# A list scheduler that knows of a port shared by VectorE and GpSimd, and one 1024-column tile of transposed exponentials in place of two of 512

## The chip, the cores and the metric

The kernel runs on one core of one Trainium2 chip. The metric is the time of one execution on the device in microseconds, as a median of runs. Engines are named as the profile names them: PE (TensorE's matmuls), PEld (its weight loads), DVE (VectorE), ACT (ScalarE), POOL (GpSimd), SP (SyncE, which here only issues DMAs).

## What is computed

```python
def _attn_ref(q, k, v, proj):            # 2 x 8 heads, 768 tokens, 64 wide
    q_bucket, k_bucket = ...             # signs of q @ proj and k @ proj, 6 bits
    mask = q_bucket[:, :, :, None] == k_bucket[:, :, None, :]
    scores = np.where(mask, scale * q @ k.T, -1e9)
    attn = np.exp(scores - scores.max(-1))
    return attn / (attn.sum(-1) + 1e-09) @ v

x = attention reshaped to 1536 x 512
x = ((x @ w1) * (x @ w2)) @ w3 @ w_out   # weights given in float64
out = sum over 4 experts of p[:, e] * (np.maximum(x @ w1[e], 0) @ w2[e])
```

The attention part is float32, and the products are made of pairs of a high part and a low part (fp32r), so that nearly every operand X is held as hi(X), a rounded copy, and lo(X) = X - hi(X).

## The kernel before, in words

The program is a list of operations, each with an engine, a duration in ns, the keys of those it depends on, and a priority. `emit_all` (the scheduler) plays this list through with a clock per engine: whichever engine is free first takes, of its operations whose inputs are there, the one with the lowest priority number, and the order that comes out is the order in which the instructions of each engine are written. On the chip each engine goes through its own list strictly in that order and waits on semaphores, so the table `RANK` (a shift of priority for each group of operations, in units of P = 5500 ns) and the durations decide who stands in front of whom.

The attention stage works on 48 **units**, one for 256 queries of one of 16 heads (three units per head). The operations of unit u are:

- `S` (PE): the scores of 128 queries against 768 keys, twice per unit, into one of two s_ps tiles.
- `mx` (DVE, L436): reads s_ps, writes e and a row minimum. `ex` (ACT, L439): exp, in place, with a row sum.
- `r1` (POOL, L452), `r2` (DVE, L454): the reciprocal of the sums. `en` (POOL L449; every fourth one on ACT, L448): scales e.
- `T` (PE, L470): 12 transposes of 128x128, in three pieces j = 0, 1, 2 of four, each into one bank of PSUM out of three (t_ps, 512 columns each).
- `hi` (ACT, L476) and `lo` (DVE, L478): read that bank and write the high and the low part of the piece into one of four et tiles. A bank is free again when `lo` of its piece is done.
- `pv` (PE): four matmuls per piece, into pv_ps. Then `po` (ACT) and `xa` (DVE for the first 27 units, POOL and a DMA afterwards) put the result into xa.

Besides that, for each head POOL prepares the hi and lo parts of q, k and v (`sc`, `h`, `l`, `vh`, `vl`: L360, L167, L170), PE and DVE make the bits for pairs of heads (`bm`, L386), and eight **conversions** run, one for each half of the four first weight tiles of the layer behind attention. `conv64` makes hi and lo parts out of float64 words: a load (`cl`), `ca` (ACT), then `c0` (L207), `c1` (L209), `c2` (L212), `c3` (L215) and `cd` (L220) on DVE, all of which read and write SBUF only, `ch` on ACT, and `cp` and `cq` on POOL (L170, L223). The priority of conversion n is C0 + n CP, so that they follow each other at equal steps. Their DVE operations carry durations of 400 and 700 ns in the scheduler where later conversions, which run with POOL idle, have 335 and 602.

From unit 38 on (`UF`) pieces rotate over two banks only, and the third (f_ps) takes the **filler**: eight chains of 12 matmuls of the next layer (`fm`), which need the converted weights, so that PE has work in the tail of attention. One of the chains uses s_ps. After attention the late stage runs from about 263 us to the end: matmul chains into u_ps and o_ps, 12 matmuls to a chain.

Of the kernel before, what the change touches and what calls it, by code (L numbers as in the profile page):

```python
# [25 lines left out]
    "C0": 16.68,  # L26
    "CP": 16.1,
    "S0": -239.52,
    "S1": 27.05,
    "T0": -88.98,  # L30
    "T1": -71.39,
    "T2": -86.81,
    "b0": -70.87,
    "b1": -163.79,
    "bits": -188.45,
    "en": -138.6,
    "ex0": 12.29,
    "ex1": -50.98,
    "fd": -30.85,
    "fx": -49.15,  # L40
    "hi0": -17.87,
    "hi1": -151.69,
    "hi2": -87.16,
    "ld": -138.95,
    "lo0": -71.6,
    "lo1": -482.92,
    "lo2": -138.58,
    "lv": -106.52,
    "mx0": -542.16,
    "mx1": -84.39,  # L50
    "p0": -19.19,
    "p1": -131.31,
    "pm": -135.95,
    "po": -194.17,
    "pr2": -131.6,
    "prep": 2.16,
    "pv": 12.21,
    "r1": -72.77,
    "r2": -255.45,
    "v": 13.17,  # L60
    "xa": -226.06,
    "xb": -108.68,
}
GROUP = {
# [10 lines left out]
def tile_lsh_attention_moe(ctx, tc, qk, v, projc, w1, w2, w3T, w_out, dp, e1, e2, out):  # L75
# [45 lines left out]
    APAD = 528  # L121
# [8 lines left out]
    NET = 4  # L130
    et_t = tiles(NET, [128, 2, 2, 256], "et", F32R)
# [16 lines left out]
    SEG = (slice(0, 512), slice(512, S))  # L148
    pv_ps = pp.tile([128, 512], F32, name="pv_ps")[:, 0:256]
    t_ps = tiles(3, [128, 512], "t_ps", p=pp)  # L150
# [3 lines left out]
    def mm(o, l, r, start, stop):  # L154
        nc.tensor.matmul(out=o, lhsT=l, rhs=r, start=start, stop=stop)  # L155
# [30 lines left out]
    def conv64(n, dst, half, src):  # L186
# [5 lines left out]
        def lo_():  # L192
# [7 lines left out]
        slow = (400, 700, 2700) if beside else (335, 602, 1460)  # L200
# [7 lines left out]
            ("DVE", slow[0], [("c0", n)], "c1",  # L208
# [5 lines left out]
            ("DVE", slow[0], [("c2", n)], "c3",  # L214
# [33 lines left out]
    def op(key, eng, dur, fn, deps, prio, group=None):  # L248
        keys[key] = len(ops)
        group = group or group_of(key)  # L250
        ops.append((eng, dur, fn, deps, prio + P * RANK.get(group, 0.0), group))

    def emit_all():
        succ = [[] for _ in ops]
        need = [0] * len(ops)
        for i, o in enumerate(ops):
            for k in set(o[3]):
                if k in keys:
                    succ[keys[k]].append(i)
                    need[i] += 1  # L260
        ready = [0.0] * len(ops)
        engines = sorted(LAT)
        free_at = {e: 0.0 for e in engines}
        wait = {e: [] for e in engines}
        avail = {e: [] for e in engines}
        for i, o in enumerate(ops):
            if not need[i]:
                heapq.heappush(wait[o[0]], (0.0, i))
        order = []
        while True:  # L270
            best = None
# [12 lines left out]
            while wait[e] and wait[e][0][0] <= t:
                i = heapq.heappop(wait[e])[1]
                heapq.heappush(avail[e], (ops[i][4], i))
            i = heapq.heappop(avail[e])[1]
            end = t + ops[i][1]
            free_at[e] = end
            order.append(i)  # L290
# [85 lines left out]
    def bits_of(ps, hs):  # L376
        for r in SEG:
            for i, hh in enumerate(hs):
                a = hh % 2
                hi, lo = hh_t[hh % HR], ll_t[hh % HR]  # L380
                mm(ps[:, r], pbh[:, a, :], hi[:, r], i == 0, False)
                mm(ps[:, r], pbl[:, a, :], hi[:, r], False, False)
                mm(ps[:, r], pbh[:, a, :], lo[:, r], False, i == len(hs) - 1)

    def is_pos(dst, ps, r, c=slice(0, S)):
        nc.vector.tensor_scalar(out=dst, in0=ps[r, c], scalar1=thr[r], scalar2=amp[r], op0=ALU.is_gt, op1=ALU.mult)  # L386

    def first_head():
# [6 lines left out]
        for i, (key, c) in enumerate(((("mq", 0), slice(0, 256)), (("sf", n), slice(256, S)))):  # L395
            op(key, "DVE", (330, 600)[i], lambda c=c: is_pos(lo[64:64 + PC, c], ps, q, c), [("mk", 0)], T + i, "b0")
# [17 lines left out]
    def unit(u):  # L414
# [6 lines left out]
        for t in range(2):  # L421
# [12 lines left out]
            op(("S", u, t), "PE", 690, score, [(k, hh) for k in ("mq", "mk", "k1", "k2", "k3", "dq")] +  # L434
               ([("sf", 0)] if 0 < u < NQ else []) + free_, Tt)
            op(("mx", u, t), "DVE", 873, lambda ps=ps, m=m, e=e: nc.vector.tensor_scalar(  # L436
                out=e, in0=ps[:, 0:S], scalar1=THR, scalar2=None, op0=ALU.min,
# [22 lines left out]
        for j in range(NJ):  # L460
            n = NJ * u + j
            ps, free_, tn = take_t(u)
            ps = ps.rearrange("p (a b) -> p a b", a=2)
            et = et_t[n % NET]

            def trans(j=j, ps=ps):
                for k in range(2):
# [7 lines left out]
            op(("T", u, j), "PE", 436, trans, en + free_, Tj)  # L475
            op(("hi", n), "ACT", 480, lambda ps=ps, et=et: nc.scalar.activation(out=et[:, 0], in_=ps, func=AF.Copy),  # L476
               [("T", u, j), ("pv", n - NET)], Tj)
            op(("lo", n), "DVE", 602, lambda ps=ps, et=et: nc.vector.tensor_tensor(  # L478
                out=et[:, 1], in0=ps, in1=f(et[:, 0]), op=ALU.subtract), [("hi", n)], Tj)
            keys[tn] = keys[("lo", n)]  # L480

        def pv(j):
            et = et_t[(NJ * u + j) % NET]
            for k in range(2):
                for p in range(2):
                    kt = 2 * j + k
                    mm(pv_ps, vv[:, kt, :], et[:, p, k, :], kt == 0 and p == 0, kt == NK - 1 and p == 1)
# [3 lines left out]
        for j in range(NJ):  # L491
            n = NJ * u + j
            op(("pv", n), "PE", 472, lambda j=j: pv(j), [("lo", n), ("vl", hh), ("xa" if u - 1 < XP else "po", u - 1), ("pv", n - 1)], Tp)
# [97 lines left out]
    def conv_tile(name, dst, fn, src, fp, after, T):  # L591
        for half in range(2):
# [3 lines left out]
            for eng, dur, deps, key, go in conv64(n, dst, half, fn(src, fp, half)):  # L596
                t = (RANK["C0"] + n * RANK["CP"]) * P if T is None else T
                hold = [("ex", CR[0] + CR[1] * n, 0)] if T is None and key == "cl" else []
                op((key, n), eng, dur, go, deps + after + hold, t - (1.5 * P if key == "cl" else 0))
# [544 lines left out]
```

## Time and profile before

| what | value |
|---|---|
| median of 3 runs | 982.67 us (982.36 to 983.55) |
| the profiled execution: its span, first to last instruction | 980.4 us |
| busy PE, DVE, ACT, POOL | 966.2, 718.6, 455.8, 200.4 us |
| mean granted TensorE clock | 1.000 |
| last `pv` ends, first chain into u_ps starts | 254.8 us, 263.3 us |

The span leaves out what lies before the first and after the last instruction of the program; the profiled execution has no other time of its own, and its span stands 2.3 us under the median of the runs. PE is busy nearly all the time by its row, but a matmul's end is modelled and matmuls overlap, so a busy PE may still be waiting a little; how much has to be counted from the spacing of its instructions.

### The profile page before, as it was taken

The numbers are of one execution on the slowest core, as the hardware profiler recorded it, in microseconds if no ns is written. First come the engines' busy times: TensorE is split into PE (matmuls) and PEld (weight loads), VectorE is DVE, ScalarE is ACT, GpSimd is POOL, SyncE is SP. The second block draws the span as 40 slices with busy tenths as digits, with TensorE's granted clock in tenths as the row PEclk, the third lists the DMA queues.
The fourth block names the chain that finished last, engine by engine and source line by source line (L and its number), as shares of the span: only waits on it lengthen the run. The fifth ranks groups of instructions, "written<-read, shape, count | busy, mean of one in ns | idle before, by whom it ended". The sixth has DMA issues, their size and how long they took to land.

```text
span 980.4 us, 14358 instructions
## 1 busy us (share of the span) xinstructions
PE 966.2 (99%) x5227; PEld 833.1 (85%) x5227; DVE 718.6 (73%) x1401; ACT 455.8 (46%) x864; POOL 200.4 (20%) x244
## 2 busy tenths in 40 slices
PE   8999999999999999999999999999999999999998
PEld 7999989888888888888888888888888888888886
DVE  7999999998599974964798745777457674476543
ACT  6999999987443422444543223322232322323121
POOL 6978878886100000000000000000000000000000
PEclk9999999999999999999999999999999999999999
DMA  6645444330133331330021102001021000200011
GB/s 171 184 124 137 114 105 116 90 92 12 54 126 113 127 108 43 110 106 1 22 65 44 44 1 84 25 22 35 9 75 34 22 24 21 64 22 1 1 65 66
DMA packets 42728, 65.58 MB, mean 67 GB/s; under 512 B 5752, under 2 KB 25784, under 8 KB 42656
## 3 DMA queue, kind: packets, MB, share of 16 engines
q1 hardware_dynamic: 42512, 64.65, 22.3%
q8 instruction: 41, 0.67, 0.3%
q14 instruction: 31, 0.25, 0.1%
q10 hardware_dynamic: 144, 0.01, 0.0%
HBM read 47.22 MB, written 3.15 MB: 51 GB/s over the span
## 4 chain that ended last, share of the span: by engine, by line
PE 86%; DVE 9%; POOL 2%; issue 1%; ACT 1%; DMA 0%; DVEq 0%; POOLq 0%; ACTq 0%
PE u_ps L155 50%; PE o_ps L155 22%; PE s_ps L155 5%; PE pv_ps L155 4%; PE t_ps L470 4%; DVE et L478 3%; DVE e L436 3%; PE t_ps L155 1%; PE t_ps L534 1%; DVE cbuf L215 0%; POOL e L449 0%; DVE xa L498 0%; DVE bt L386 0%; DVE cbuf L207 0%; ACT et L476 0%
## 5 line engine op out<-in xcount | busy, mean ns | idle before, releaser
L155 PE MATMUL o_ps<-slotl,hl 128*128 128x512 f32 x768 | 180.0, 390 | 0.0
L155 PEld LDWEIGHTS o_ps<-slotl,hl 128*128 128x128 f32 x768 | 142.9, 188 | 28.9
L155 PE MATMUL u_ps<-xh,slotl 128*128 128x512 f32 (+1 forms) x672 | 137.2, 359 | 0.0
L155 PEld LDWEIGHTS u_ps<-xh,slotl 128*128 128x128 f32 x672 | 114.3, 189 | 18.7
L155 PE MATMUL u_ps<-xh,slot 128*128 128x512 f32 (+1 forms) x576 | 116.8, 353 | 0.0
L155 PEld LDWEIGHTS u_ps<-xh,slot 128*128 128x128 f32 x576 | 97.8, 189 | 16.6
L951 DVE TENSOR_TENSOR m<-m,u_ps 128x512 f32<-128x512 f32 x96 | 63.2, 682 | 62.1 <-PE u_ps L155 60.8
L478 DVE TENSOR_TENSOR et<-t_ps,et 128x512 fp32r<-128x512 f32 x144 | 96.4, 680 | 4.8 <-ACT et L476 4.3
L439 ACT ACTIVATE e<-e,sm 128x768 f32<-128x768 f32 x96 | 89.8, 938 | 10.4 <-DVE e L436 9.7
L436 DVE TENSOR_SCALAR_CACHE_REDUCE e<-s_ps 128x768 f32<-128x768 f32 x96 | 90.4, 945 | 2.1 <-PE t_ps L470 1.0
L155 PE MATMUL pv_ps<-et,vv 128*128 128x256 f32 x576 | 89.3, 294 | 0.9 <-DVE xa L498 0.4
L470 PE MATMUL t_ps<-ident,e 128*128 128x128 f32 x576 | 84.2, 274 | 4.3 <-DVE et L478 3.9
L155 PE MATMUL u_ps<-slotl,hl 128*128 128x512 f32 x384 | 87.7, 389 | 0.0
L476 ACT ACTIVATE et<-t_ps 128x512 fp32r<-128x512 f32 x144 | 82.1, 595 | 9.9 <-PE t_ps L470 5.8
L155 PEld LDWEIGHTS u_ps<-slotl,hl 128*128 128x128 f32 x384 | 72.1, 188 | 15.0
L470 PEld LDWEIGHTS t_ps<-ident,e 128*128 128x128 f32 x576 | 66.0, 140 | 13.2 <-DVE et L478 5.6
L155 PEld LDWEIGHTS pv_ps<-et,vv 128*128 128x128 f32 x576 | 74.3, 190 | 2.0 <-DVE xa L498 0.6
L449 POOL TENSOR_SCALAR e<-e,sm 128x768 f32<-128x768 f32 x72 | 65.9, 922 | 8.1 <-DVE sm L454 5.7
L946 DVE SCALAR_TENSOR_TENSOR hl<-gl,hl 128x512 fp32r<-128x512 f32 x32 | 22.1, 692 | 47.7 <-ACT hl L1088 47.7
L943 ACT ACTIVATE hl<-m 128x512 fp32r<-128x512 f32 x32 | 20.3, 633 | 76.6 <-DVE m L951 76.6
L161 ACT ACTIVATE m<-u_ps 128x512 f32<-128x512 f32 x32 | 19.1, 598 | 79.0 <-issue 61.9
L155 PE MATMUL s_ps<-ka,hh 128*128 128x512 f32 x192 | 52.8, 356 | 3.1 <-DVE e L436 2.5
(157 smaller groups left out, 1563.0 us busy)
## 6 DMA issues: line engine op xcount, KB each, us to landing
wraw<-in_e SPq DMA_DIRECT2D x64, 256.0 KB
wraw<-in_w SPq DMA_DIRECT2D x16, 512.0 KB
wraw<-in_w3T SPq DMA_DIRECT2D x16, 512.0 KB
r<-in_qk SPq DMA_DIRECT2D x15, 384.0 KB
wraw<-in_w_out SPq DMA_DIRECT2D x8, 512.0 KB
rv<-in_v SPq DMA_DIRECT2D x16, 192.0 KB
ka<-hh SPq DMA_DIRECT2D x15, 192.0 KB
kb<-hh SPq DMA_DIRECT2D x15, 192.0 KB
```

The source lines that it names most:

```text
L155: nc.tensor.matmul(out=o, lhsT=l, rhs=r, start=start, stop=stop)
L161: nc.scalar.activation(out=dst, in_=ps, func=AF.Copy)
L436: op(("mx", u, t), "DVE", 873, lambda ps=ps, m=m, e=e: nc.vector.tensor_scalar(out=e, in0=ps[:, 0:S], scalar1=THR, scalar2=None, op0=ALU.m ...
L439: op(("ex", u, t), "ACT", 921, lambda e=e, m=m, rs=rs: nc.scalar.activation(out=e, in_=e, func=AF.Exp, scale=-1.0, bias=m, accum_out=rs), ...
L449: return "POOL", 872, lambda: nc.gpsimd.tensor_scalar(out=e, in0=e, scalar1=r[:, t:t + 1], scalar2=1.0, op0=ALU.mult, op1=ALU.mult)
L470: nc.tensor.transpose(out=ps[:, k, t * 128:(t + 1) * 128], in_=e_t[2 * (u % ER) + t][:, kt * 128:(kt + 1) * 128], identity=ident)
L476: op(("hi", n), "ACT", 480, lambda ps=ps, et=et: nc.scalar.activation(out=et[:, 0], in_=ps, func=AF.Copy), [("T", u, j), ("pv", n - NET)], Tj)
L478: op(("lo", n), "DVE", 602, lambda ps=ps, et=et: nc.vector.tensor_tensor(out=et[:, 1], in0=ps, in1=f(et[:, 0]), op=ALU.subtract), [("hi", ...
L534: nc.tensor.transpose(out=t_ps[i % 2][:, 0:128], in_=ident, identity=ident)
L943: op(key, "ACT", 480, lambda: nc.scalar.activation(out=hl_t[n % 2][:, 0], in_=m_t[m], func=AF.Relu), after, clock[0])
L946: op(key, "DVE", 602, lambda: nc.vector.scalar_tensor_tensor(out=hl_t[n % 2][:, 1], in0=src(), scalar=0.0, in1=f(hl_t[n % 2][:, 0]), op0=A ...
L951: nc.vector.tensor_tensor(out=out, in0=a, in1=b, op=o)
```

## The change

Three things change together, all in the attention stage.

1. **The port rule.** Every operation gets a mark whether it uses the port that DVE and POOL share: on DVE those of the set `TWO_PORT` (the conversions' operations, and a few others that read only SBUF), on POOL everything but two set-up operations. In `emit_all`, while a marked operation of one of the two engines runs, the other one starts no marked operation: it takes its best unmarked one, or, where there is none, waits until the port is free or until another operation becomes ready. The conversions' DVE durations drop from 400 and 700 to 335 and 602.
2. **The wide tile.** For units below 38, the pieces j = 0 and 1 become one piece of eight transposes into t_x, one PSUM tile of 1024 columns (two banks), read by one `hi` and one `lo` of 1024 columns. Piece 2 goes to t_y, the third bank. There is one t_x and one t_y. Of the SBUF tiles, two of [128, 2, 4, 256] (etx) and one of [128, 2, 2, 256] (ety) replace four of [128, 2, 2, 256]. From unit 38 on the pieces are three of four transposes again, over the halves of t_x.
3. **The table.** All values of `RANK` are new, and each of the eight conversions has a value of its own (cv0 to cv7) in place of C0 + n CP. The duration of `S` goes from 690 to 703, that of `pv` from 472 to 480.

Instructions are the same but for these: 38 `hi` and 38 `lo` of 1024 columns stand in place of 76 each of 512. The line numbers move: `hi` is L519, `lo` L521, `mx` L469, `T` L513 in the changed kernel, and c0, c1, c2, c3, cd are L223, L225, L228, L231, L236.

```diff
 RANK = {
-    "C0": 16.68,
-    "CP": 16.1,
...
+    "cv6": 77.14,
+    "cv7": 1027.95,
...
+TWO_PORT = {"c0", "c1", "c2", "c3", "cd", "cp", "cq", "k1", "l", "xl", "pb", "pr"}
...
-    et_t = tiles(NET, [128, 2, 2, 256], "et", F32R)
+    ex_t = tiles(2, [128, 2, 4, 256], "etx", F32R)
+    ey_t = tiles(1, [128, 2, 2, 256], "ety", F32R)
...
-    t_ps = tiles(3, [128, 512], "t_ps", p=pp)
+    t_x = pp.tile([128, 1024], F32, name="t_x")
+    t_ps = [t_x[:, 0:512], t_x[:, 512:1024], pp.tile([128, 512], F32, name="t_y")]
...
-        slow = (400, 700, 2700) if beside else (335, 602, 1460)
+        slow = (335, 602, 2700, 335, 335) if beside else (335, 602, 1460, 335, 335)
...
+        shares = key[0] in TWO_PORT if eng == "DVE" else eng == "POOL" and key[0] not in ("id", "zc")
...
+            pick = 0
+            held = port[{"DVE": "POOL", "POOL": "DVE"}[e]] if e in port else 0.0
+            if held > t:
+                pick = next((k for k, (_, i) in enumerate(avail[e]) if not ops[i][6]), None)
+                if pick is None:
+                    if wait[e]:
+                        held = min(held, max(t, wait[e][0][0]))
+                    if held > t:
+                        free_at[e] = held
+                        continue
+                    pick = 0
+            i = avail[e].pop(pick)[1]
...
+        wide = u < UF
+        pieces = ((0, 4), (2, 2)) if wide else ((0, 2), (1, 2), (2, 2))
+        for j, w in pieces:
             n = NJ * u + j
+            if wide:
+                ps = t_x if w == 4 else t_ps[2]
+                free_ = [("lo", n - NJ)] if u else []
+            else:
+                ps, free_, tn = take_t(u)
...
-            op(("T", u, j), "PE", 436, trans, en + free_, Tj)
...
-               [("T", u, j), ("pv", n - NET)], Tj)
-            op(("lo", n), "DVE", 602, lambda ps=ps, et=et: nc.vector.tensor_tensor(
...
+            op(("T", u, j), "PE", 218 * w, trans, en + free_, Tj)
+            op(("hi", n), "ACT", 480 if w == 2 else 907, lambda ps=ps, et=et_of: nc.scalar.activation(out=et()[:, 0], in_=ps, func=AF.Copy),
+               [("T", u, j)] + busy, Tj)
+            op(("lo", n), "DVE", 602 if w == 2 else 1136, lambda ps=ps, et=et_of: nc.vector.tensor_tensor(
...
-                t = (RANK["C0"] + n * RANK["CP"]) * P if T is None else T
```

What this does to the order is shown at three places. **First, DVE around units 29 and 30**, where a conversion runs beside POOL (cbuf is the conversions' tile, et the split pieces, e the scores, bt the bits). Before:

```order
L436 TENSOR_SCALAR e3_100,sm1_124<-s_ps1_131 128x768
L478 TENSOR_TENSOR et2_105<-t_ps0_133,et2_105 128x512
L386 TENSOR_SCALAR bt_114<-s_ps0_130,thr_121,amp_122 128x768
L212 SCALAR_TENSOR_TENSOR cbuf_71<-wraw0_69,cbuf_71 128x512
L207 TENSOR_SCALAR cbuf_71<-cbuf_71 128x512
L436 TENSOR_SCALAR e4_101,sm5_128<-s_ps1_131 128x768
L454 RECIPROCAL sm4_127<-sm4_127 128x2
L478 TENSOR_TENSOR et3_106<-t_ps1_134,et3_106 128x512
```

With the change:

```order
L546 TENSOR_TENSOR xa_72<-pv_ps_131,pvs0_106 64x256
L228 SCALAR_TENSOR_TENSOR cbuf_71<-wraw1_70,cbuf_71 128x512
L521 TENSOR_TENSOR etx0_103<-t_x_132,etx0_103 128x1024
L418 TENSOR_SCALAR bt_113<-s_ps0_129,thr_120,amp_121 128x768
L469 TENSOR_SCALAR e4_101,sm5_127<-s_ps1_130 128x768
L487 RECIPROCAL sm4_126<-sm4_126 128x2
L231 TENSOR_SCALAR cbuf_71<-cbuf_71 128x512
L546 TENSOR_TENSOR xa_72<-pv_ps_131,pvs1_107 64x256
```

Conversion operations no longer stand back to back here: between c2 and c3 there are now operations that read PSUM. Over the whole stage the 40 of them are spread anew; c0 of the first stands behind 12 `mx` in place of 22, and the last two cd stand behind all 96 `mx` (before, the last one stood behind 92).

**Second, ACT around units 30 to 33** (e and sm belong to `ex`, pvs to `po`, et to `hi`). Before, a unit's three `hi` stand between other operations:

```order
L439 ACTIVATE e0_97,sm3_126<-e0_97,sm3_126 128x768
L448 ACTIVATE e5_102<-e5_102,sm2_125 128x768
L476 ACTIVATE et0_103<-t_ps1_134 128x512
L476 ACTIVATE et1_104<-t_ps2_135 128x512
L496 ACTIVATE pvs0_107<-pv_ps_132 64x256
L439 ACTIVATE e1_98,sm3_126<-e1_98,sm3_126 128x768
L476 ACTIVATE et2_105<-t_ps0_133 128x512
```

With the change one wide `hi` stands between two `ex`, and the narrow one behind `po`:

```order
L472 ACTIVATE e0_97,sm0_122<-e0_97,sm0_122 128x768
L519 ACTIVATE etx0_103<-t_x_132 128x1024
L472 ACTIVATE e1_98,sm0_122<-e1_98,sm0_122 128x768
L551 ACTIVATE pvs0_106<-pv_ps_131 128x256
L519 ACTIVATE ety0_105<-t_y_133 128x512
L472 ACTIVATE e2_99,sm1_123<-e2_99,sm1_123 128x768
L519 ACTIVATE etx1_104<-t_x_132 128x1024
```

The next unit's wide `hi` reads the same t_x, so one wide piece has to be through ACT and DVE before PE may write the next.

**Third, PE at the end of attention** (pv_ps is the last unit's, s_ps and the tile left of slot2 and slot3 are filler chains). Before:

```order
L155 MATMUL t_ps2_135<-xh0_66,slot2_64 128x512 x4
L155 MATMUL pv_ps_132<-et3_106,vv1_96 128x256 x4
L155 MATMUL t_ps2_135<-xh0_66,slot2_64 128x512 x3
L155 MATMUL s_ps0_130<-xh0_66,slot2_64 128x512 x5
L155 MATMUL t_ps2_135<-xh0_66,slot3_65 128x512 x12
L155 MATMUL s_ps0_130<-xh0_66,slot2_64 128x512 x6
```

With the change:

```order
L171 MATMUL s_ps0_129<-xh0_66,slot2_64 128x512
L171 MATMUL pv_ps_131<-ety0_105,vv1_96 128x256 x4
L171 MATMUL t_y_133<-xh0_66,slot3_65 128x512 x12
L171 MATMUL s_ps0_129<-xh0_66,slot2_64 128x512 x6
L171 MATMUL t_y_133<-xh0_66,slot3_65 128x512 x12
L171 MATMUL u_ps0_2994<-xh1_67,slot0_62 128x512 x12
```

Of the 96 filler matmuls 66 stand ahead of the last `pv` and 30 behind it, where there were 58 and 38; the chain on slot3, which reads the last two conversions, follows the last `pv` at once.

## Rows read from the trace of the kernel before

**Rows 1.** The page: the span
```profile
span 980.4 us, 14358 instructions
```

**Rows 2.** Busy time in two stretches of attention (us, instructions of each engine)
```profile
25.00:100.00 75.00, 74.28 (x547) 68.86 (x546) 72.90 (x157) 71.82 (x142) 62.74 (x76) 1.00 0.54 145
100.00:225.00 125.00, 120.08 (x862) 109.09 (x860) 124.23 (x248) 113.26 (x228) 105.50 (x124) 1.00 0.38 101
```

**Rows 3.** Chain that ended last, in order of time: start, us, what
```profile
28.69 1.31 PE t_ps L470 x12
...
96.81 1.41 PE s_ps L155 x8
...
99.18 1.44 PE pv_ps L155 x12
...
168.01 2.79 PE s_ps L155 x16
...
260.70 2.72 PE t_ps L155 x12
```

**Rows 4.** PE matmuls into pv_ps, busy and count, in the two stretches
```profile
25.00:100.00 75.00, 28.54 (x191) 1.00 0.54 145
100.00:225.00 125.00, 46.22 (x302) 1.00 0.38 101
```

**Rows 5.** PE transposes (L470) in the two stretches
```profile
25.00:100.00 75.00, 27.93 (x192) 1.00 0.54 145
100.00:225.00 125.00, 42.96 (x292) 1.00 0.38 101
```

**Rows 6.** PE matmuls into s_ps in the two stretches
```profile
25.00:100.00 75.00, 34.22 (x164) 1.00 0.54 145
100.00:225.00 125.00, 50.84 (x244) 1.00 0.38 101
```

**Rows 7.** PE matmuls into t_ps, transposes and filler, in the second stretch
```profile
100.00:225.00 125.00, 48.80 (x316) 1.00 0.38 101
```

**Rows 8.** Groups of DVE, 0 to 263 us: count, busy us, mean ns, idle before
```profile
L478 DVE TENSOR_TENSOR et<-t_ps,et 128x512 fp32r<-128x512 f32 x144 | 96.4, 680 | 4.8 <-ACT et L476 4.3
L436 DVE TENSOR_SCALAR_CACHE_REDUCE e<-s_ps 128x768 f32<-128x768 f32 x96 | 90.4, 945 | 2.1 <-PE t_ps L470 1.0 <-PE s_ps L155 0.8
...
L220 DVE SCALAR_TENSOR_TENSOR cbuf<-wraw,cbuf 128x512 f32<-128x512 uint32 x8 | 7.4, 925 | 0.0
L212 DVE SCALAR_TENSOR_TENSOR cbuf<-wraw,cbuf 128x512 int32<-128x512 int32 x8 | 7.3, 912 | 0.0
L215 DVE TENSOR_SCALAR cbuf<-cbuf 128x512 int32<-128x512 int32 x8 | 7.2, 898 | 0.0
L207 DVE TENSOR_SCALAR cbuf<-cbuf 128x512 f32<-128x512 f32 x8 | 6.6, 829 | 0.0
```

**Rows 9.** The same DVE groups, 263 to 480 us, where POOL has no work
```profile
L220 DVE SCALAR_TENSOR_TENSOR cbuf<-wraw,cbuf 128x512 f32<-128x512 uint32 x32 | 22.1, 689 | 0.7
...
L215 DVE TENSOR_SCALAR cbuf<-cbuf 128x512 int32<-128x512 int32 x32 | 13.6, 425 | 0.8
...
L207 DVE TENSOR_SCALAR cbuf<-cbuf 128x512 f32<-128x512 f32 x32 | 13.4, 420 | 0.3 <-ACT cbuf L205 0.3
```

**Rows 10.** Timeline: one conversion operation and the POOL operation beside it
```profile
147.52 1.85 POOL L170 TENSOR_TENSOR ll<-r,hh 128x768 fp32r<-128x768 f32 x1
...
147.92 1.73 DVE L215 TENSOR_SCALAR cbuf<-cbuf 128x512 int32<-128x512 int32 x1
```

**Rows 11.** Timeline of DVE: three `lo` in a row
```profile
19.44 1.89 DVE L478 TENSOR_TENSOR et<-t_ps,et 128x512 fp32r<-128x512 f32 x3 [0.35 <-ACT et L476]
```

**Rows 12.** Groups of ACT, 0 to 263 us
```profile
L439 ACT ACTIVATE e<-e,sm 128x768 f32<-128x768 f32 x96 | 89.8, 938 | 10.4 <-DVE e L436 9.7 <-DVE sm L454 0.3
L476 ACT ACTIVATE et<-t_ps 128x512 fp32r<-128x512 f32 x144 | 82.1, 595 | 9.9 <-PE t_ps L470 5.8 <-PE pv_ps L155 2.9
...
L503 ACT ACTIVATE pvs<-pv_ps 128x256 f32<-128x256 f32 x21 | 8.0, 381 | 2.1 <-PE pv_ps L155 2.1
```

More of the change, by code (lines that the diff above doesn't have):

```diff
@@ L1 @@
 import heapq
+from bisect import insort
 from contextlib import ExitStack
@@ L25 @@
 RANK = {
-    "C0": 16.68,
-    "CP": 16.1,
[L28 to L62, printed above, removed]
+    "S0": -423.92,
+    "S1": 69.62,
+    "T0": 71.72,
+    "T1": 245.99,
+    "T2": -280.82,
+    "b0": -43.10,
+    "b1": 123.46,
+    "bits": -410.97,
+    "cv0": 127.60,
+    "cv1": 137.76,
+    "cv2": 255.75,
+    "cv3": 229.99,
+    "cv4": -70.71,
+    "cv5": 243.77,
+    "cv6": 77.14,
+    "cv7": 1027.95,
+    "en": 76.92,
+    "ex0": 59.99,
+    "ex1": 110.62,
+    "fd": 123.24,
+    "fx": 173.01,
+    "hi0": -411.79,
+    "hi1": -518.41,
+    "hi2": -376.52,
+    "ld": 180.17,
+    "lo0": -412.69,
+    "lo1": 52.91,
+    "lo2": -211.06,
+    "lv": 126.38,
+    "mx0": -351.00,
+    "mx1": -67.19,
+    "p0": 143.74,
+    "p1": -68.61,
+    "pm": -388.46,
+    "po": -391.84,
+    "pr2": 122.14,
+    "prep": 277.91,
+    "pv": 71.73,
+    "r1": -420.66,
+    "r2": -342.00,
+    "v": 303.68,
+    "xa": -103.78,
+    "xb": 424.14,
 }
+TWO_PORT = {"c0", "c1", "c2", "c3", "cd", "cp", "cq", "k1", "l", "xl", "pb", "pr"}
 GROUP = {
@@ L263, in emit_all @@
         free_at = {e: 0.0 for e in engines}
+        port = {"DVE": 0.0, "POOL": 0.0}
         wait = {e: [] for e in engines}
@@ L376, in bits_of @@
     def bits_of(ps, hs):
-        for r in SEG:
+        for w, r in SEG:
             for i, hh in enumerate(hs):
@@ L394, in first_head @@
         op(("mk", 0), "DVE", 930, lambda: is_pos(kb[k], ps, k), [("bm", -1)], T, "b0")
-        for i, (key, c) in enumerate(((("mq", 0), slice(0, 256)), (("sf", n), slice(256, S)))):
-            op(key, "DVE", (330, 600)[i], lambda c=c: is_pos(lo[64:64 + PC, c], ps, q, c), [("mk", 0)], T + i, "b0")
+        pieces = ((slice(0, 256),) * 2, (slice(256, S),) * 2)
+        for i, (key, c) in enumerate(((("mq", 0), pieces[0]), (("sf", n), pieces[1]))):
+            op(key, "DVE", (330, 600)[i], lambda c=c: is_pos(lo[64:64 + PC], ps, q, c), [("mk", 0)], T + i, "b0")
     def pair(p):
@@ L459, in unit, with et_of, trans @@
         NJ = NK // 2
-        for j in range(NJ):
+        wide = u < UF
+        pieces = ((0, 4), (2, 2)) if wide else ((0, 2), (1, 2), (2, 2))
+        for j, w in pieces:
             n = NJ * u + j
[L462 to L467, printed above, removed]
+            if wide:
[3 more added lines that the diff above has]
+                ps, free_, tn = take_t(u)
+            ps = ps.rearrange("p (a b) -> p a b", a=w)
+            def et_of(j=j, w=w):
+                return ey_t[0] if j == 2 else ex_t[u % 2][:, :, 2 * j:2 * j + w]
+            busy = [("pv", n - NJ)] if j == 2 else [("pv", NJ * (u - 2) + i) for i in range(2)]
+            def trans(j=j, ps=ps, w=w):
+                for k in range(w):
                     for t in range(2):
```

68 lines of the change are left out of this document (39 added, 29 removed).

## The prediction

> **What bounds the kernel now.** I read the chain of waits first, then the busy times by stretch, then the groups of single engines, and last the timeline beside one of the suspected waits. The change touches the attention stage alone, the first 263 of 980.4 us [rows 1]; behind it every instruction but its line number is as before, in PE's chains of 12 matmuls at 2.72 us each [rows 3], so what attention gains or loses should pass to the end nearly one to one.
>
> In attention the question is what holds PE up. The chain shows what PE's pieces cost where they run without a gap: 12 transposes 1.31 us, 8 score matmuls 1.41, 12 `pv` matmuls 1.44, 12 filler matmuls 2.72 [rows 3]. That is 109, 176, 120 and 227 ns apiece, and 4.16 us per unit. The stretch of 16 score and bit matmuls (2.79 us) is 174 each, so I take 175 for all into s_ps. PE's need in a stretch is then its counts times these:
>
> - 25 to 100 us: 191 x 0.120 + 192 x 0.109 + 164 x 0.175 = 22.9 + 20.9 + 28.7 = 72.5 us [rows 4 to 6]. PE has nothing to do for 2.5 of 75 us.
> - 100 to 225 us: 302 x 0.120 + 292 x 0.109 + 244 x 0.175 + 24 x 0.227 (316 matmuls into t_ps less 292 transposes) = 36.2 + 31.8 + 42.7 + 5.4 = 116.1 us [rows 4 to 7]. PE idles for 8.9 of 125 us.
>
> So PE is the floor, and 11.4 us in these 200 us are all that any new order could give back there. Who takes them? In the second stretch DVE is busy for 124.23 of 125 us, ACT for 113.26, POOL for 105.50 [rows 2]. DVE is what PE waits for there, and part of DVE's time is no work: a conversion's c3 takes 898 ns beside POOL [rows 8] and 425 where POOL is silent [rows 9]. The timeline shows the mechanism: c3 starts at 147.92 and lasts 1.73 us, until 149.65, while a POOL operation runs from 147.52 to 149.37 [rows 10]. It waited for POOL's end and then did its 0.4 us.
>
> **The change part by part.**
>
> *Port rule: the prize.* The waits cost 8 x (925 - 689) + 8 x (898 - 425) + 8 x (829 - 420) = 1.9 + 3.8 + 3.3 = 9.0 us for cd, c3 and c0 [rows 8, 9]; c2 (912) has cd's form, alone some 689, which gives 1.8 more. 10.8 us of DVE, nearly all in the second stretch. The new order puts operations that read PSUM beside POOL, and the conversions where POOL pauses. If all of it went, DVE would fall to some 91% there, and PE would be the bound. I do not take the full 8.9 us, since the order is fixed beforehand: a POOL operation that comes 0.5 us late meets the conversion after all. I take it that the second stretch becomes as tight as the first, in which few conversions run: 2.5 / 75 of idle, or 4.2 of 125 us. **-4.7 us**, between 0 (the waits return elsewhere) and -8.9.
>
> *The wide tile, on the engines.* Three `lo` in a row take 1.89 us, and the last of them 0.68, so one costs 0.605 in a row [rows 11, 8]. No row shows 1024 columns. From 512 (680) and 768 columns (945, another operation that reads PSUM) 256 columns more cost 265 ns [rows 8], so a wide `lo` lasts an estimated 1.21 us, and 1.135 in a row. Two narrow ones: 1.21. That saves DVE 75 ns a unit, 38 x 0.075 = 2.9 us. On ACT, 256 columns cost 595 and 381 ns at 512 and 256 columns, 214 more [rows 12]; the wide `hi` is then some 1.02 us, and the saving a similar 0.1 us at most. On the path this counts where DVE is the bound and the first term has not taken the idle away: the first stretch, 16 units x 0.075 = 1.2 of its 2.5 us; I take half. **-0.6 us**, between 0 and -1.2.
>
> *The wide tile, as a loop.* There is one t_x. Its next transposes wait for `lo` of the unit before, so each unit needs eight transposes (0.87), the wide `hi` (1.02), the wide `lo` (1.21) and some 0.3 of hand-overs: 3.4 us in a row. A unit takes 75 / (191 / 12) = 4.71 us now [rows 4]. 1.3 us is left for standing behind other work: behind one `ex` (938) or one `mx` (945) [rows 8, 12], not behind both. Before, a piece of four needed half of each and had as long. The order shows the wide `hi` between two `ex` of ACT, behind the first by rule. I take **0**, since one of the two waits fits, and keep a cost to +10.8 as a rival below. etx has two copies and `pv` runs a unit behind, so SBUF adds no wait of its own; ety has one, freed by the third `pv` of the unit before, which stands just behind these transposes on PE, ahead of `hi`.
>
> *POOL's side of the port.* Where DVE goes first, POOL waits now: 40 conversion operations of some 0.5 us, 20 us, against POOL's 105.5 of 125 us [rows 2]. POOL's `en` feeds the transposes. Some of this existed before. Between 0 and +2; I take **+0.6**.
>
> *Head, tail and queues.* The filler moves: 8 more of its matmuls stand ahead of the last `pv`, worth 8 x 0.227 = 1.8 us if they land in gaps. Against that, the last conversions end later, and the chain on slot3 stands directly behind the last `pv` where 2.7 us of other filler covered it: with that cover gone, a late `cq` on POOL stops PE. Both of about 1.8 us; I take **0**, from -1.8 to +2. Loads on SP keep their count and the unit at which each may start, and a load of 1460 to 2700 ns has several units of lead. Conversions moved forward to units 6 to 12 add DVE work to a stretch in which DVE has 2 us left [rows 2]: in the first term already, which takes the two stretches at one pace.
>
> **Sum:** -4.7 - 0.6 + 0 + 0.6 + 0 = -4.7 us on the profiled execution, whose span is 980.4. The median, 982.67, stands 2.3 us over it for what lies around the span, and that does not change: 982.7 - 4.7 = **978.0 us**.
>
> **The rivals.**
>
> 1. *The loop through t_x becomes the bound* (slower). If the wide piece finds both ACT and DVE taken, a unit lasts 3.4 + 0.94 + 0.945 = 5.28 us, 0.57 over today's. In every second unit ACT has one `en` more, the likeliest place: 19 x 0.57 = 10.8 us, less the 4.7 gained: 988.8 us. It decides from 1.3 us of waiting per unit on. For it: ACT is at 113 of 125 us and DVE at 124 [rows 2], so both are nearly always taken. Against it: in the rows of the order one `ex` stands ahead of the wide `hi`, not two, and `pv`, scores and a narrow piece (some 3.3 us of PE's work) stand between two wide pieces anyway. 0.13. The Trainium skill speaks for this one: "Trainium Kernel Development and Optimization", section Best Practices, wants buffers doubled, and takes regular bubbles as a sign that SBUF or PSUM has run out; by it one t_x alone would cost more than one bank fewer in a rotation. No run here shows it yet.
> 2. *The wait only changes hands* (no change). POOL's 105.5 us and the conversions' 18 or so in the second stretch fill its 125 us [rows 2, 9]; if the port itself is what is full, DVE's gain is POOL's loss, and `en` comes late. Then the first term is 0 and the rest cancels: 982.2 us. For it: the sum of the two. Against: part of POOL's busy time is itself waiting for DVE, and the new order takes conversions out of the second stretch into both ends. 0.18. That a POOL operation blocks just as fully when it comes second is what "SBUF - State Buffer" of the Trainium skill says in its part on the shared port pair, an exclusive lock for a whole instruction; the 1.73 us of c3 agree for the one direction [rows 10].
> 3. *All of it comes back.* PE runs through: -8.9 and -1.2 and part of the tail: 972.6 us. For it: PE's floor is real, and DVE and ACT are both relieved. Against: even the first stretch leaves 2.5 us. 0.14.
>
> **How the numbers follow.** The forecast has the remaining 0.55. About 0.2%, 2 us, is what a measurement of this kernel tells from no change, so "same" is 980.7 to 984.6. Forecast and rival 3 are faster: 0.69; rival 2 is the same: 0.18; rival 1 is slower: 0.13. The range goes from nearly rival 3 to over rival 2, 972 to 984.5, and leaves out rival 1 and what lies below 972. The forecast's own range is 974 to 980.5.
>
> **What would show it.** c0, c2, c3 and cd in attention nearer to 420 and 689 than to 829 and 898 (say a mean below 600 for c3); PE's need over 225 us of attention unchanged, but the last `pv` near 250 in place of 254.8 and the first chain into u_ps near 258.5 in place of 263.3; DVE in the second stretch below 97%. The wide `lo` near 1.21 us and the wide `hi` near 1.02. Rival 1 would show PE waiting on `lo` ahead of t_x, 0.5 us a unit; rival 2 short conversions, but longer `en`, `l` and `xa` on POOL and transposes that wait for `en`. I am wrong if attention ends after 262, or if the late stage changes by more than 1 us.

## The result, and the profile after

The changed kernel takes **994.62 us** (994.27 to 996.34, 4 runs), the one before 982.93 us beside it (982.36 to 983.55, 4 runs): ratio 1.012 (95% interval 1.0108 to 1.0133), slower by 1.2%. The forecast was 978.0 us, in a range of 972.0 to 984.5. The profiled execution has a span of 992.6 us against 980.4, so 12.2 us have to be found.

The page of the changed kernel, its span and busy times:

```profile
span 992.6 us, 14194 instructions
## 1 busy us (share of the span) xinstructions
PE 969.4 (98%) x5227; PEld 831.4 (84%) x5227; DVE 710.5 (72%) x1363; ACT 452.3 (46%) x826; POOL 199.4 (20%) x244
```

DVE's busy time fell from 718.6 to 710.5 us, ACT's from 455.8 to 452.3, and yet PE, which does the same work, needs 12 us more. First the second stretch of [rows 2], in the changed kernel (columns as there: length, then busy us and instructions of PE, PEld, DVE, ACT, POOL, the granted clock):

```profile
100.00:225.00 125.00, 120.87 (x870) 109.89 (x867) 114.75 (x223) 111.50 (x207) 95.55 (x118) 1.00 0.38 96
```

DVE has room now: 92% of the second stretch where it had 99%. This stretch does not show where the loss is, because it runs into the tail. So I cut anew where the units end. Up to 64 us, from there to the last `pv` of unit 37 (201.8), and on to 263.4; first before, then after:

```profile
0.00:64.00 64.00, 60.07 (x408) 54.68 (x409) 55.10 (x124) 52.68 (x100) 50.43 (x64) 1.00 0.64 169
64.00:201.80 137.80, 134.65 (x986) 124.07 (x985) 136.90 (x285) 129.58 (x260) 114.87 (x139) 1.00 0.43 111
201.80:263.40 61.60, 58.91 (x382) 51.80 (x382) 46.20 (x84) 43.50 (x88) 35.06 (x42) 1.00 0.17 52
```

```profile
0.00:64.00 64.00, 57.59 (x383) 50.94 (x384) 52.50 (x112) 48.72 (x84) 48.77 (x63) 0.97 0.59 160
64.00:201.80 137.80, 136.64 (x1012) 126.72 (x1011) 131.04 (x253) 128.48 (x236) 113.35 (x139) 1.00 0.43 110
201.80:263.40 61.60, 52.26 (x334) 42.96 (x332) 43.67 (x86) 40.05 (x79) 35.77 (x42) 1.00 0.16 45
```

PE's matmul counts show where work is late: 25 fewer in the first stretch, 26 more in the second, 48 fewer in the third. In time, by the ends of the units' last `pv`:

| part of the run | before, us | after, us | difference |
|---|---|---|---|
| start to the end of unit 8 | 64.1 | 67.2 | +3.1 |
| units 9 to 37 (wide tile) | 137.8 | 134.5 | -3.3 |
| units 38 to 47 (three narrow pieces) | 52.9 | 65.1 | +12.2 |
| last `pv` to the first chain into u_ps | 8.5 | 6.6 | -1.9 |
| late stage | 717.1 | 719.1 | +2.0 |

The sum is +12.1. So units 9 to 37, which have the wide tile, the port rule and the new table together, got faster; which of the three did it is not shown by this. The loss is for the most part in the ten units without the wide tile, and smaller losses stand at the start and in the late stage.

**What the tail does.** The chain that ended last, of the changed kernel, in its tail (start us, us, what):

```profile
208.58 0.67 PE t_x L513 x4
209.34 0.70 DVE etx L521
210.07 0.61 ACT etx L519
...
210.81 0.64 PE t_x L513 x4
211.54 0.70 DVE etx L521
212.27 0.61 ACT etx L519
212.92 0.67 PE t_x L513 x4
213.69 0.70 DVE etx L521
214.41 0.61 ACT ety L519
215.06 0.66 PE t_x L513 x4
```

The PE pieces are transposes (T), those of DVE `lo`, those of ACT `hi`. The timeline of the same microseconds, PE, DVE and ACT, with each engine's idle time and what ended it in brackets:

```profile
208.58 0.66 PE L513 MATMUL t_x<-ident,e 128*128 128x128 f32 x4 [0.28 <-ACT etx L519]
...
210.81 0.63 PE L513 MATMUL t_x<-ident,e 128*128 128x128 f32 x4 [0.62 <-ACT etx L519]
...
212.92 0.66 PE L513 MATMUL t_x<-ident,e 128*128 128x128 f32 x4 [0.78 <-ACT etx L519]
```

```profile
209.34 0.69 DVE L521 TENSOR_TENSOR etx<-t_x,etx 128x512 fp32r<-128x512 f32 x1 [1.40 <-PE t_x L513]
```

```profile
207.95 0.57 ACT L519 ACTIVATE etx<-t_x 128x512 fp32r<-128x512 f32 x1
210.07 0.60 ACT L519 ACTIVATE etx<-t_x 128x512 fp32r<-128x512 f32 x1 [1.54 <-DVE etx L521]
```

Read it as a relay with one baton. The transposes at 208.58 write one half of t_x, and end at 209.24. The `lo` at 209.34 belongs to the piece before, whose `hi` ran at 207.95, and reads the *other* half; it waits for these transposes all the same. The `hi` of the new piece could start at 209.24 and starts at 210.07, when that `lo` of the other half is done. The next transposes, at 210.81, wait for that `hi`. T, `lo`, `hi`, T, `lo`, `hi`, never two at once: from 208.58 to 215.06 three pieces, 2.16 us each. The tail's 30 pieces took 65.1 us, 2.17 us each on average, but not all of them run in this step: behind 215.06 the steps between PE's transposes vary, up to 4.1 us, and other operations come into the chain. So the loop is what the tail falls into where nothing else holds it up, and its share of the 12.2 us has to come from experiments. PE's waits from 201 to 264 us (engine, line waited for: us in total, times, longest) are mostly of this kind:

```profile
PE t_x L513 <- DVE etx L521: 3.4, 5, 1.3
PE t_x L513 <- ACT etx L519: 2.4, 6, 0.8
```

With those that end with ety or sm they come to 9.3 us, where the kernel before has 2.7 us of waits.

The two halves are one tile, t_x. The reading that e1 and e2 below test is that the program puts whatever touches a tile in the order in which it was written, whichever half it touches. The scheduler's list knows nothing of that: there a bank is free when `lo` of its own piece is done. Before, t_ps were three tiles.

**What went as forecast.** The conversions' groups of DVE up to 263 us, which answer to [rows 8], and the wide operations:

```profile
L521 DVE TENSOR_TENSOR etx<-t_x,etx 128x1024 fp32r<-128x1024 f32 x38 | 46.3, 1219 | 8.8 <-ACT etx L519 8.7
...
L236 DVE SCALAR_TENSOR_TENSOR cbuf<-wraw,cbuf 128x512 f32<-128x512 uint32 x8 | 6.3, 794 | 0.0
...
L228 DVE SCALAR_TENSOR_TENSOR cbuf<-wraw,cbuf 128x512 int32<-128x512 int32 x8 | 6.1, 769 | 0.0
L231 DVE TENSOR_SCALAR cbuf<-cbuf 128x512 int32<-128x512 int32 x8 | 5.0, 624 | 0.0
L223 DVE TENSOR_SCALAR cbuf<-cbuf 128x512 f32<-128x512 f32 x8 | 4.1, 520 | 0.0
```

c3 fell from 898 to 624 ns, c0 from 829 to 520, cd from 925 to 794, c2 from 912 to 769: of the 10.8 us put down to the port, 8 x (274 + 309 + 131 + 143) ns = 6.9 us are gone. The wide `lo` takes 1219 ns (1.21 was the estimate), and the wide `hi` 1015 (1.02), by ACT's groups:

```profile
L519 ACT ACTIVATE etx<-t_x 128x1024 fp32r<-128x1024 f32 x38 | 38.6, 1015 | 2.8 <-PE t_x L513 2.8
```

### The profile page after: what moved, and what is told of

Same layout as the page of the kernel before. It is cut to its first block, busy times and chain, and to the rows that moved or that the text cites. A ratio compares the mean times of both kernels' runs of the same rounds, so it can differ in the third digit from the quotient of the medians.

```text
span 992.6 us, 14194 instructions
## 1 busy us (share of the span) xinstructions
PE 969.4 (98%) x5227; PEld 831.4 (84%) x5227; DVE 710.5 (72%) x1363; ACT 452.3 (46%) x826; POOL 199.4 (20%) x244
## 4 chain that ended last, share of the span: by engine, by line
PE 84%; DVE 7%; ACT 5%; issue 1%; POOL 1%; DMA 0%; SPq 0%; DVEq 0%; ACTq 0%; POOLq 0%
PE u_ps L171 49%; PE o_ps L171 21%; PE s_ps L171 5%; PE pv_ps L171 4%; PE t_x L513 3%; DVE etx L521 2%; ACT etx L519 2%; ACT e L472 2%; DVE e L469 2%; PE t_y L513 1%; ACT ety L519 1%; PE t_y L171 1%; DVE ety L521 1%; ACT e L481 0%; DMA r<-in_qk 0%
## 5 line engine op out<-in xcount | busy, mean ns | idle before, releaser
L171 PEld LDWEIGHTS u_ps<-xh,slot 128*128 128x128 f32 x576 | 97.6, 189 | 16.4
L469 DVE TENSOR_SCALAR_CACHE_REDUCE e<-s_ps 128x768 f32<-128x768 f32 x96 | 90.2, 946 | 2.8 <-PE t_x L513 2.2
L521 DVE TENSOR_TENSOR etx<-t_x,etx 128x1024 fp32r<-128x1024 f32 (+1 forms) x58 | 60.0, 1036 | 22.5 <-ACT etx L519 11.8
L482 POOL TENSOR_SCALAR e<-e,sm 128x768 f32<-128x768 f32 x72 | 68.8, 964 | 13.4 <-DVE sm L487 7.7
L513 PE MATMUL t_x<-ident,e 128*128 128x128 f32 x424 | 58.4, 275 | 12.0 <-DVE etx L521 5.6
L513 PEld LDWEIGHTS t_x<-ident,e 128*128 128x128 f32 x424 | 46.9, 140 | 22.3 <-DVE etx L521 4.4
L171 PE MATMUL pv_ps<-etx,vv 128*128 128x256 f32 x384 | 57.6, 290 | 0.5 <-DVE etx L521 0.4
L519 ACT ACTIVATE etx<-t_x 128x1024 fp32r<-128x1024 f32 (+1 forms) x58 | 50.4, 871 | 16.6 <-PE t_x L513 10.0
L171 PEld LDWEIGHTS pv_ps<-etx,vv 128*128 128x128 f32 x384 | 49.5, 189 | 2.5 <-DVE etx L521 0.7
```

Source lines behind the costliest of these rows:

```text
L482: return "POOL", 872, lambda: nc.gpsimd.tensor_scalar(out=e, in0=e, scalar1=r[:, t:t + 1], scalar2=1.0, op0=ALU.mult, op1=ALU.mult)
L513: nc.tensor.transpose(out=ps[:, k, t * 128:(t + 1) * 128], in_=e_t[2 * (u % ER) + t][:, kt * 128:(kt + 1) * 128], identity=ident)
L519: op(("hi", n), "ACT", 480 if w == 2 else 907, lambda ps=ps, et=et_of: nc.scalar.activation(out=et()[:, 0], in_=ps, func=AF.Copy), [("T", ...
L521: op(("lo", n), "DVE", 602 if w == 2 else 1136, lambda ps=ps, et=et_of: nc.vector.tensor_tensor(out=et()[:, 1], in0=ps, in1=f(et()[:, 0]), ...
```

## The experiments

Two theories stood at first. A: the halves of t_x being one tile makes the tail's loop. B: the new order is itself bad in the tail, where the last conversions come late. Each kernel was timed beside the kernel before, which took 982.73 us with e1 to e4 and 982.41 with e5 to e8; the ratios are to that, with their 95% intervals.

### e1: two separate tiles in the tail

The changed kernel, with its order on every engine, but at unit 38 t_x is given up and two tiles of 512 columns take its two banks.

```diff
-    t_x = pp.tile([128, 1024], F32, name="t_x")
-    t_ps = [t_x[:, 0:512], t_x[:, 512:1024], pp.tile([128, 512], F32, name="t_y")]
...
+    t_x = tp.tile([128, 1024], F32, name="t_x")
...
+    def part():
+        t_stack.close()
+        np_ = attn_stack.enter_context(tc.tile_pool(name="attn_tn", bufs=1, space=PSUM, reuse_waits="tile"))
+        t_n.extend(tiles(2, [128, 512], "t_n", p=np_))
```

> The changed kernel, instruction for instruction in its order; only the place of the narrow pieces differs: at unit 38 the tile of 1024 columns is given up and two tiles of 512 take its two banks. Theory A (from unit 38 on the two halves are one tile, so that a transpose into one half waits for the readers of the other half): PE no longer waits for hi and lo of the neighbouring piece, the ten last units take about 53 us as in the kernel before in place of 65, and the median falls by 10 to 13 us to 981 to 985. Theory B (the new order itself is bad in the tail, because the last conversions were moved there and fill DVE and POOL): nothing that sets the order has changed, so the median stays at 993 to 996.

Measured: **981.71 us** (980.83 to 982.81), ratio 0.999 [0.9981, 0.9998]. With not one instruction in another place, 12.9 us are gone; taken each against the kernel before beside it (11.7 us over, then 1.0 under), 12.7. The tail took 52.3 us. Its timeline on PE, over the same work as above (t_n are the new tiles):

```profile
207.89 0.60 PE L527 MATMUL t_n<-ident,e 128*128 128x128 f32 x4
...
209.28 0.60 PE L527 MATMUL t_n<-ident,e 128*128 128x128 f32 x4
...
210.41 0.60 PE L527 MATMUL t_n<-ident,e 128*128 128x128 f32 x4
...
211.80 0.60 PE L527 MATMUL t_n<-ident,e 128*128 128x128 f32 x4
```

Three pieces now take 3.91 us where they took 6.48, and no row has a wait; from 201 to 264 us PE waits once, for 0.8 us. A is shown; B falls, since the order is the same. The SBUF tile etx, whose two halves are also written piece by piece in the tail, is still one tile here; what was shown is for the PSUM tile.

### e2: the kernel before, with two of its three tiles as halves of one

```diff
-    t_ps = tiles(3, [128, 512], "t_ps", p=pp)
+    t_x = pp.tile([128, 1024], F32, name="t_x")
+    t_ps = [t_x[:, 0:512], t_x[:, 512:1024], pp.tile([128, 512], F32, name="t_y")]
```

Again no instruction is moved.

> The kernel before, instruction for instruction in its order; only two of its three 512-column PSUM tiles for transposed e become halves of one tile of 1024 columns. Theory A: now all 48 units have pieces that wait for the neighbouring half; a lockstep step took 2.15 us in the changed kernel's tail, and with one of three pieces in a tile of its own a unit would go from 4.7 to 5.2 to 6 us: 24 to 60 us slower, 1005 to 1045. Theory B: no instruction and no order differs, 982 to 984.

Measured: **1015.89 us** (1015.66 to 1017.3), ratio 1.0335 [1.0319, 1.035]. One declaration costs 33 us. Among the waits of that kernel up to 290 us:

```profile
ACT et L477 <- DVE et L479: 20.0, 25, 2.3
...
DVE et L479 <- PE t_x L471: 17.3, 27, 1.5
...
PE t_x L471 <- DVE et L479: 12.4, 17, 1.7
PE t_x L471 <- ACT et L477: 11.1, 25, 1.3
```

A `lo` that waits for transposes is the mark of the fault: a `lo` comes after its own `hi`, which comes after its own transposes, so the transposes it waits for are another piece's. In the kernel before the 144 `lo` sat idle for 4.8 us in all, 4.3 of them for ACT [rows 8]. The ten last units took 65.9 us in e2, near the changed kernel's 65.1, though the order is that of the kernel before: the loss in the tail comes with the shared tile, and not with the order.

### e3 and e5: three narrow tiles everywhere, with the new rule and table

In e3 the changed kernel makes three narrow pieces in every unit, on three tiles as before.

```diff
-        wide = u < UF
+        wide = False
```

> The changed kernel with its port rule, its table and its durations, but with three pieces of 512 columns in three tiles for every unit, as before the change; the scheduler makes its own order of that. Theory A: no shared tile, no lockstep in the tail; the table was not made for this, so 976 to 986. Theory B: the tail has the same late conversions, so 988 to 996.

Measured: **1029.63 us** (1027.75 to 1031.18), ratio 1.0474 [1.046, 1.0489]. Both theories missed. Units 9 to 37 took 174.8 us in place of 134.5 in the changed kernel. The longest of its waits:

```profile
POOL sm L484 <- ACT e L471: 40.0, 33, 4.2
```

I took it that the table's three values for the middle piece were to blame, which only the last ten units of the changed kernel use. e5 gives them those of the first piece:

```diff
-    "T1": 245.99,
+    "T1": 71.72,
...
-    "hi1": -518.41,
+    "hi1": -411.79,
...
-    "lo1": 52.91,
+    "lo1": -412.69,
```

> The three narrow tiles everywhere with the new table and rule (the run before this at 1029.6 us), but the table's three values of the middle piece (transposes 245.99, hi -518.41, lo 52.91) set to those of the first piece (71.72, -411.79, -412.69). Theory P: those three values are what was slow, since only the last ten units of the changed kernel go by them and nothing tied them to the others: 975 to 990 us, PE's idle time between 25 and 225 us falls from 28 to under 12 us. Rival Q: three narrow tiles stay slow under this rule and table, whatever the middle piece's values: over 1015 us.

Measured: **1001.34 us** (1000.95 to 1001.56), ratio 1.0193 [1.018, 1.0207]. Between the two theories: the three values were worth 28 us, and 19 over the kernel before are left. So most of what e3 lost says nothing about narrow tiles: three numbers that served ten units did not serve all 48. What the other 19 us come from was not found.

### e4, e6 and e7: one part of the change at a time

e4 is the kernel before with the port rule and the rule's durations, its old table and tiles:

```diff
-            i = heapq.heappop(avail[e])[1]
+            pick = 0
+            held = port[{"DVE": "POOL", "POOL": "DVE"}[e]] if e in port else 0.0
...
+            i = avail[e].pop(pick)[1]
```

> The kernel before with the port rule and its shorter conversion durations alone, old table, old tiles. Theory A says nothing against it: the waits of conversions for POOL get shorter (a mean for c3 well below 898 ns), and the time lies between 976 and 986, the order being new and no table made for it. Theory B: 986 or more, because the rule holds POOL or DVE back where the time is short.

Measured: **991.24 us** (991.02 to 991.43), ratio 1.0085 [1.0071, 1.0098]. By its DVE groups c3 and c0 got shorter (704 and 451 ns) and c2 and cd did not (937 and 996), and the time is longer: it lies in theory B's range, though whether B's reason is the cause was not tested. By the ends of the units, the first nine units lost 5.0 us (unit 0 alone 3.7), units 9 to 37 4.5, and 5.8 went between the last `pv` and the first chain into u_ps; units 38 to 47 were 6.3 us shorter.

e6 is e1 with the rule off and the durations of before:

```diff
-            if held > t:
+            if False:
...
-        slow = (335, 602, 2700, 335, 335) if beside else (335, 602, 1460, 335, 335)
+        slow = (400, 700, 2700, 400, 400) if beside else (335, 602, 1460, 335, 335)
```

> The changed kernel with separate tiles in the tail (981.7 us), with the port rule off and the conversions' planned durations put back to 400 and 700, its new table kept. Theory R: the rule itself keeps the conversions away from POOL; without it c3 is again near 900 ns, units 8 to 37 take 137 to 139 us in place of 134.5, the whole 984 to 988. Rival S: the table alone does that (it places each conversion of its own), c3 stays near 640 and the time within 2 us of 981.7.

Measured: **1005.5 us** (1004.02 to 1005.8), ratio 1.0231 [1.0217, 1.0245]. Slower than either theory said. The conversions in its DVE groups:

```profile
L245 DVE SCALAR_TENSOR_TENSOR cbuf<-wraw,cbuf 128x512 f32<-128x512 uint32 x8 | 8.3, 1038 | 0.0
L237 DVE SCALAR_TENSOR_TENSOR cbuf<-wraw,cbuf 128x512 int32<-128x512 int32 x8 | 8.1, 1011 | 0.0
L232 DVE TENSOR_SCALAR cbuf<-cbuf 128x512 f32<-128x512 f32 x8 | 6.2, 778 | 0.0
...
L240 DVE TENSOR_SCALAR cbuf<-cbuf 128x512 int32<-128x512 int32 x8 | 4.1, 524 | 0.0
```

The rows are cd, c2, c0 and c3. The first three are long again, c3, which theory R had named, is not: so R agrees with three of the four, and the time misses both theories. In e1 the four took 813, 773, 589 and 643 ns; in e6 they take 8 x (1038 + 1011 + 778 + 524 - 813 - 773 - 589 - 643) ns = 4.3 us more, a small part of the 23.8 us that e6 lost against e1. The trace has the loss in units 9 to 37: 160.0 us in place of 134.5.

e7 is e1 with the table, the conversions' places and the durations of before, and the rule off: the wide tile without the rest of the change.

```diff
-    "T0": 71.72,
+    "T0": -88.98,
...
-                op((key, n), eng, dur, go, deps + after + hold, (T or 0) - (1.5 * P if key == "cl" else 0),
-                   f"cv{n}" if T is None else None)
+                op((key, n), eng, dur, go, deps + after + hold, ((RANK["C0"] + n * RANK["CP"]) * P if T is None else T) - (1.5 * P if key == "cl" else 0))
```

> Wide tile up to unit 37 and separate tiles after, with the table, the conversions' places and durations of before and no port rule: the wide tile alone. Theory W: the wide tile costs nothing as a loop and gives 0.075 us of DVE a unit at most: 980 to 985 us, the late stage as long as before. Rival L: one wide tile without a second copy is a loop of some 3.4 us that stands behind ACT and DVE, 0.3 to 0.6 us a unit: 990 to 1005 us.

Measured: **1011.02 us** (1008.71 to 1011.62), ratio 1.0288 [1.0274, 1.0302]. Outside both again. PE did wait for the wide `lo`, but more for something else. From the waits of that kernel, the long ones of PE and its weight loads (PEld):

```profile
PEld s_ps L174 <- DVE e L472: 19.3, 21, 2.5
...
PE s_ps L174 <- DVE e L472: 13.6, 14, 2.2
...
PE t_x L521 <- DVE etx L529: 8.5, 14, 1.8
```

The larger part is scores that wait for `mx`, so the loop through t_x is not the main loss in this order. But 8.5 us in 14 waits for the wide `lo` are left, and rival L is not excluded by this.

e3 to e7 belong together. Rule, pieces and table were each taken out or put in without the others, and each time the kernel was 8.5 to 47 us slower than the one before. My reading, which e5 supports and no run shows, is that a table fits one set of rule and pieces, so that switching one part measures a misfit. What the rule, the wide tile and the table are each worth by themselves stays open; a fitted table for each would be needed, which was not tried. Only what keeps the order of attention as it is (e1, e2 and the next) prices one thing.

### e8: the late stage's two microseconds

The kernels with the new table (the changed one, e1, e3, e5, e6) took 718.9 to 719.4 us from the first chain into u_ps to the end, those with the old one (before, e2, e4, e7) 717.1 to 717.2. The changed kernel has one long wait of PE in it, which the kernel before does not have (zs is an operand of the late stage):

```profile
499.85 2.88 PE L171 MATMUL o_ps<-slotl,hl 128*128 128x512 f32 x12
504.08 1.66 PE L171 MATMUL u_ps<-slot,zs 128*128 128x512 f32 x6 [1.35 <-DVE m L999]
```

The table's `b1` stands for a group of attention operations, but an addition of the late stage has the same name: `mix("b1", ...)`, 16 operations of DVE on m. The change moved b1 from -163.79 to 123.46, and the late addition along with it, by 287 steps of P. e8 is e1 with the old value for the late one:

```diff
+    "b1late": -163.79,
...
+        if k == "b1":
+            k = "b1late"
```

> The kernel with separate tiles in the tail (981.7 us) with one number more: the table's b1, meant for a group of the attention stage, is also the name of an addition of the late stage (m, on DVE, 16 of them), which the change so moved by 287 steps; here these get the value of before, -163.79. Every engine's attention order stays as it was. Theory N: the late stage's 2.0 to 2.3 us extra come from that: PE's gap of 1.35 us ahead of the chain of zs goes, first chain into u_ps to the end 717 us, the whole 979.2 to 980.2. Rival: the late stage stays at 719 us and the whole at 981.7.

Measured: **979.54 us** (979.02 to 982.0, 7 runs), ratio 0.9975 [0.9964, 0.9985]. In the profiled execution the late stage takes 978.1 - 260.7 = 717.4 us, and the gap is gone:

```profile
486.05 1.52 PE L181 MATMUL u_ps<-slotl,slotl 128*128 128x512 f32 x6
487.40 1.52 PE L181 MATMUL u_ps<-slot,zs 128*128 128x512 f32 x6
```

Theory N is shown, and e8 is faster than both kernels: 0.25% under the one before, and 14.6 us under the changed one when each is taken against the kernel before beside it (2.9 us under, 11.7 over), with two repairs of a few lines.

## Why the prediction was wrong

**The step that failed** stands under *Head, tail and queues*: "Both of about 1.8 us; I take **0**, from -1.8 to +2." It weighed filler matmuls and the last conversions, and did not look at the pieces of units 38 to 47 at all, though the change turns their banks from tiles into halves of a tile. The pieces that it left out measured +12.2 us in the trace, and 12.7 us by e1. No row of the kernel before shows that two halves of a tile act as one buffer, but the rows could price it: four transposes (0.44 us), one `hi` of 595 ns [rows 12], one `lo` of 680 [rows 8] and 0.3 of hand-overs in a row are an estimated 2.0 us a piece, or 60 us for 30 pieces, against 52.9 us that the tail had. What was missing was the question of who else touches the same tile.

**The second failed sentence** is that behind attention "every instruction but its line number is as before"; nor do the changes stand "all in the attention stage", as the list of them has it. One name in the table reached into the late stage: +2.0 us, and e8 took 1.9 back. Both named signs of being wrong came: the late stage changed by more than 1 us, and attention ended after 262 (the last `pv` at 266.8 us).

These two are 12.7 + 1.9 = 14.6 of the 16.4 us between the -4.7 forecast and the +11.7 measured.

**Port rule, -4.7 us.** The mechanism is borne out in part, and its reach was short. DVE's share fell below 97% and c3 came down, to 624 ns where I said under 600. I took it that the second stretch would become as tight as the first: in the trace PE did 26 more matmuls in the same 137.8 us, and units 9 to 37 gained 3.3 us, rule, wide tile and table together, against 4.7 + 0.6 forecast for the whole stage. The row that the mechanism was read from does not fit it to the end either: c3 ends 0.28 us behind the POOL operation [rows 10], less than the 0.425 us that it takes alone. What was not priced is the start. Unit 8 ends 3.1 us later, and e8, with both faults repaired, keeps that loss (67.2 us). Between 8 and 68 us PE's waits come to 4.2 us in the changed kernel and 2.3 in the one before; three of their places, in PE's timeline of the changed kernel:

```profile
22.90 1.06 PE L513 MATMUL t_x<-ident,e 128*128 128x128 f32 x8 [0.96 <-DVE etx L521]
...
52.01 0.61 PE L171 MATMUL s_ps<-ka,hh 128*128 128x512 f32 x2 [0.85 <-DVE e L469]
...
57.32 0.85 PE L513 MATMUL t_x<-ident,e 128*128 128x128 f32 x6 [0.90 <-DVE etx L521]
```

I had put the conversions that move to units 6 to 12 "in the first term already"; that was too kind. What makes the start slower was not taken apart.

**Wide tile on the engines, -0.6.** Its sizes were right to 1%, 1219 and 1015 ns. What it is worth by itself stays open (e7).

**Rival 1** forecast the right side for the wrong reason. It had the loop through the *wide* t_x at 0.57 us in every second unit. Two of the places above (22.90, 57.32), where transposes into t_x wait for the wide `lo`, are that loop, for 1.9 us, early in the stage. Units 9 to 37 are faster as a whole, so it did not decide there. The loop that decided is the narrow one behind it, on the same banks. The sentence of the Trainium skill that I had beside it, in "Trainium Kernel Development and Optimization", Best Practices, says that consistent bubbles can mean that SBUF or PSUM has run out. Bubbles came in the tail, 0.28 to 0.78 us ahead of the pieces shown; but no bank was short, since e1 has the same two banks and none of these bubbles.

**Rival 2** (the wait changes hands) did not happen as a whole: POOL's busy time from 64 to 201.8 us fell too, from 114.87 to 113.35. One of its signs came: `en` on POOL took 964 ns on average where it took 922. What POOL's side cost (+0.6) was not measured by itself. The sum of this rival was off: with the first term at 0 and the rest cancelling it comes to 982.7, not 982.2. **Rival 3** needed the whole idle time back, and in units 9 to 37 3.3 us came.

**The tail's other half** came out better than 0: the chain on slot3 directly behind the last `pv` did not stop PE, and last `pv` to first u_ps fell from 8.5 to 6.6 us, the 1.9 us that more filler ahead of the last `pv` was to be worth (1.8).

## What to carry to other kernels

When two buffers become halves of one tile, look up everyone who uses the halves apart, also in stages that the change is not about: where the program orders accesses by tile, they become one buffer. The mark in a profile is a reader that waits for the writer of a piece it does not read, and, where nothing else holds the loop up, a period that is the sum of the loop's operations and hand-overs (0.66 + 0.69 + 0.60 us of the 2.16 here). And where a table of priorities sets the order, a part is priced cleanly only by an edit that leaves the order alone; other edits may measure how badly the table fits. Search for the table's names outside the stage it is meant for.

## What the runs showed of the hardware that was not expected

TensorE's clock fell early in the profiled execution of the changed kernel, and cost nothing that the trace shows. Granted clock and busy times in slices of 5 us (columns as above):

```profile
10.00:15.00 5.00, 3.92 (x18) 2.69 (x18) 4.71 (x10) 2.87 (x6) 2.35 (x4) 0.94 0.79 236
15.00:20.00 5.00, 4.90 (x26) 3.95 (x25) 3.25 (x7) 3.33 (x8) 4.58 (x7) 0.72 0.54 132
```

A matmul of 512 columns into s_ps took 630 ns at 14.49 us there, and 400 at the same place in e8, which kept 1.00: the lower of the two levels, 1.2 in place of 2.4 GHz, which with shares of 0.94 and 0.72 makes some 3.4 us in all. Ahead of the fall PE had been busy for 4.38 of the 5 us up to 10 us; in e8 and before for 5.00. Yet the transposes that follow start at 22.90 us in the changed kernel and at 22.88 in e8: both wait there for DVE, 0.96 and 1.05 us. The slow PE only shortened the waits that stood between: at 18.88 us e8's transposes wait 1.07 us for POOL, and the changed kernel's, at 18.62, for nothing.

The wide operations cost what the prediction had worked out from narrower ones: 1219 ns against 679 to 688 for 512 columns on DVE, 1015 against 598 on ACT. One operation of 1024 columns saves 0.15 us on DVE and 0.18 on ACT over two of 512 by their means, or 5.6 and 6.9 us of busy time for 38 of each; what of that reached PE is not shown.
